# Each expert job of a mixture in two halves, with a branch of its own for each half

## The chip, the cores and the metric

The kernel runs on one core of one Trainium2 chip. The metric is the device time of one execution in microseconds (us). The time of a kernel is the median of its runs.

## The reference

Linear attention is followed by two mixtures of experts; the second takes the output of the first. The change touches the first mixture alone.

```
def _moe_ref(x, w_gate, w1, w2, capacity):        # x 1152 x 512, 8 experts, w1 512 x 1024, w2 1024 x 512
    logits = x @ w_gate
    expert_idx = np.argmax(logits, axis=1)        # one expert for each token
    ...
    disp = np.zeros((E, capacity, D))             # capacity 288 rows for each expert
    ...
    h = np.maximum(np.einsum('ecd,edf->ecf', disp, w1), 0.0)
    y = np.einsum('ecf,efd->ecd', h, w2)
    ...
    out[i] = gate_w[i] * y[expert_idx[i], pos[i]]
```

How many tokens an expert gets is known only when the gate has been computed on the chip.

## The kernel before

Every float32 operand is kept as two parts, a high one (names with H) and a low one (L), and each product is made by `three()` with three matmuls, on lines 198 to 200: high by high, high by low, low by high. All engines run programs of their own, and each engine's program has its own branches.

**The jobs.** The first mixture is a loop over 8 experts (lines 803 to 818), unrolled in the program. Each expert is a job, and each job stands in the program twice, one after the other: as a wide job for up to 288 tokens (`job_wide`) and as a narrow one for up to 128 (`job_narrow`). On each engine a compare-and-branch on the number of tokens (line 810) either goes on into the wide arm, at whose end an unconditional branch jumps over the narrow arm, or jumps over the wide arm to the narrow one. With the inputs of the runs the jobs are, in order, wide, wide, narrow, narrow, wide, narrow, narrow, narrow (the wide ones have matmuls of 288 columns, the narrow ones of 256). Behind the last job a branch of the same kind (line 1133) leads to the second mixture, of which two versions stand in the program.

**A wide job.** The first product has 8 blocks of 128 hidden features, each 4 x 3 matmuls into one PSUM bank; ScalarE evicts a block to `h1H` (line 586), VectorE to `h1L` (line 587). The second product has 4 blocks of 8 x 3 matmuls, which are evicted to `x2H` and `x2L`; behind each of the first three come transposes of the next job's tokens (`win_T`, line 668, 3 matmuls for each of 4 column blocks, from `xw` to `x1H`, `x1L`).

**A narrow job** has the operands of the matmuls swapped, so that tokens come out as rows. The first product has 4 groups of 12 matmuls of 128 x 256; ScalarE evicts each to `hn` (line 724). `turn_h` transposes `hn` back, 4 matmuls of line 715 for groups 0 and 1 (behind the last group), and 4 for groups 2 and 3; they are split into `h1H` and `h1L` (lines 193, 194). Between the two stand `win_T` for column blocks 0 and 1. The second product has 2 groups of 24 matmuls, `win_T` of blocks 2 and 3, the load of the tokens of the job after the next (`win_load`, line 660, one DMA of 576 KB from `xe` to `xw`), and 4 transposes of the result (line 753).

So the wide arm has 96 + 96 + 12 = 204 matmuls, the narrow arm 48 + 4 + 6 + 4 + 48 + 6 + 4 = 120. In the program of TensorE a matmul is two instructions, a weight load and a multiplication.

**Weights.** `wt.split` turns one raw tile of an expert's weights into its two parts (lines 155 and 158; ScalarE makes the high part, VectorE or GpSimd the low one) and then issues the DMA of the next expert's tile into the same raw tile. A job splits the `w1H`, `w1L` that its own second product needs during its first product, and the next job's `w0H`, `w0L` during its second.

**PSUM.** `bank()` hands out the banks of a ring of five in turn (`ring["n"]` counts). Both arms start with the same count, and go on after it with the wide arm's.

Of the kernel before, what the change touches and what calls it, by code (L numbers as in the profile page):

```python
# [20 lines left out]
def kernel(  # L21
# [18 lines left out]
    E, _, F = moe_w1.shape  # L40
    P = 128
# [70 lines left out]
    ring = {"use": pb[0:4], "n": 0}  # L112

    def bank(n):
        ring["n"] += 1
        return ring["use"][ring["n"] % len(ring["use"])][:, 0:n]
# [75 lines left out]
    def split2(hi, lo, src):  # L192
        nc.scalar.activation(out=hi, in_=src, func=AF.Copy)
        nc.vector.tensor_tensor(out=lo, in0=src, in1=hi.bitcast(F32), op=ALU.subtract)

    def three(ps, a, b, i, n):
        (aH, aL), (bH, bL) = a, b
        nc.tensor.matmul(ps, lhsT=aH, rhs=bH, start=i == 0, stop=False)  # L198
        nc.tensor.matmul(ps, lhsT=aH, rhs=bL, start=False, stop=False)  # L199
        nc.tensor.matmul(ps, lhsT=aL, rhs=bH, start=False, stop=i == n - 1)  # L200
# [382 lines left out]
    def evict_split(hi, lo, ps, relu=False):  # L583
        if not relu:
            return split2(hi, lo, ps)
        nc.scalar.activation(out=hi, in_=ps, func=AF.Relu)
        nc.vector.scalar_tensor_tensor(
            out=lo, in0=ps, scalar=0.0, in1=hi.bitcast(F32), op0=ALU.max, op1=ALU.subtract)
# [20 lines left out]
    def wide(t):  # L609
        return t.rearrange("p (a f) -> p a f", f=P)  # L610

    def operands(g):
        return tuple(wide(t) for t in sp0[4 * (g % 2):4 * (g % 2) + 4])

    def prep(g, tmp=None):
        e, p = divmod(g, 4)
        sH, sL, aH, aL = operands(g)
        r = wt.raw[0, p].rearrange("p a (b h f) -> p (a b) h f", h=2, f=P)
        a11, a12, a21, a22 = r[:, 0:2, 0, :], r[:, 2:4, 0, :], r[:, 0:2, 1, :], r[:, 2:4, 1, :]
        parts = [(slice(0, 4), r[:, :, 0, :])] + (  # L620
            [(slice(4, 6), a22)] if g else [(slice(4, 8), r[:, :, 1, :])])
        tt = nc.gpsimd.tensor_tensor
        for o, w in parts:
            nc.scalar.activation(out=aH[:, o, :], in_=w, func=AF.Copy)  # L624
        if g:
            s1, s2, s3, s4 = (wide(tmp)[:, 2 * k:2 * k + 2, :] for k in range(4))
            tt(out=s1, in0=a21, in1=a22, op=ALU.add)
            tt(out=s2, in0=s1, in1=a11, op=ALU.subtract)
        yield
        if g:  # L630
            tt(out=s3, in0=a11, in1=a21, op=ALU.subtract)
            tt(out=s4, in0=a12, in1=s2, op=ALU.subtract)
        yield
        for o, w in parts:
            tt(out=aL[:, o, :], in0=w, in1=aH[:, o, :].bitcast(F32), op=ALU.subtract)  # L635
        if g:
            nc.scalar.activation(out=sH, in_=wide(tmp), func=AF.Copy)
        yield
        if g:
            tt(out=sL, in0=wide(tmp), in1=sH.bitcast(F32), op=ALU.subtract)  # L640
        yield

    with ExitStack() as mctx:
# [9 lines left out]
        def win_load(j):  # L653
            if j >= len(jobs):
                return
            e, w = jobs[j]
            r0 = e * CW + w * W
            step = P if j == 0 else DM
            for o in range(0, DM, step):
                nc.sync.dma_start(  # L660
                    out=xw[:, :, o:o + step], in_=xe[r0:r0 + W, o:o + step].rearrange("(a p) d -> p a d", p=WP))

        def win_T(j, c):
            if j >= len(jobs):
                return
            ps = bank(W)
            for a in range(3):
                nc.tensor.transpose(  # L668
                    ps[:, a * WP:(a + 1) * WP], xw[:, a, c * P:(c + 1) * P], ident[0:WP, 0:WP])
            split2(*x1[c], ps)  # L670

        def job_wide(j, off_r):
            i, w = jobs[j]
            for kk, f in enumerate(FO):
                ps = bank(W)
                for c in range(NC):
                    three(ps, wt.w1(f, c), x1[c], c, NC)
                evict_split(h1H[:, kk, :], h1L[:, kk, :], ps, relu=True)
                if i > 0 and kk < 4 and w == 0:
                    wt.split(i, 1, kk)  # L680
            pg = prep(0)
            for d in range(NC):
                ps = bank(W)
                for kk, f in enumerate(FO):
                    wH, wL = wt.w2(f)
                    three(ps, (wH[:, d * P:(d + 1) * P], wL[:, d * P:(d + 1) * P]),
                          (h1H[:, kk, :], h1L[:, kk, :]), kk, NFC)
                evict_split(x2H[:, d, ds(off_r, W)], x2L[:, d, ds(off_r, W)], ps)
                for c in ((0, 1), (2,), (3,), ())[d]:
                    win_T(j + 1, c)  # L690
                if d == 2:
                    win_load(j + 2)
                if w == NW - 1:
                    if i + 1 < E:
                        wt.split(i + 1, 0, d)
                    else:
                        next(pg)

        def job_narrow(j, off_r):
            i, w = jobs[j]  # L700
            pool = {(1, 3), (0, 1), (0, 3)}

            pg = prep(0)

            def split(i, which, p):
                if i == E:
                    next(pg)
                else:
                    wt.split(i, which, p, nc.gpsimd if (which, p) in pool else None)

            def turn_h(g):
                ps = bank4()
                for f in range(4):
                    o = f % 2 * P
                    nc.tensor.transpose(ps[:, f, :], hn[2 * g + f // 2][:, o:o + P], ident)
                split2(h1H[:, 4 * g:4 * g + 4, 0:P], h1L[:, 4 * g:4 * g + 4, 0:P], ps)

            if i > 0:
                split(i, 1, 0)
            for p in range(4):  # L720
                ps = bank(256)
                for c in range(NC):
                    three(ps, (x1[c][0][:, 0:P], x1[c][1][:, 0:P]), wt.w1p(p, c), c, NC)
                nc.scalar.activation(out=hn[p], in_=ps, func=AF.Relu)
                if i > 0 and p < 3:
                    split(i, 1, p + 1)
                if p == 1:
                    ring["n"] += 1
                if p == 2:
                    turn_h(0)  # L730
            win_T(j + 1, 0)
            win_T(j + 1, 1)
            turn_h(1)
            ring["n"] += 1
            split(i + 1, 0, 0)
            split(i + 1, 0, 1)
            for g in range(2):
                ps = bank(256)
                for kk, f in enumerate(FO):
                    wH, wL = wt.w2(f)  # L740
                    n = slice(g * 256, (g + 1) * 256)
                    three(ps, (h1H[:, kk, 0:P], h1L[:, kk, 0:P]), (wH[:, n], wL[:, n]), kk, NFC)
                nc.scalar.activation(out=yn[g], in_=ps, func=AF.Copy)
                if g == 0:
                    win_T(j + 1, 2)
                    split(i + 1, 0, 2)
            win_T(j + 1, 3)
            win_load(j + 2)
            ring["n"] += 1
            ps = bank4()  # L750
            for c in range(NC):
                o = c % 2 * P
                nc.tensor.transpose(ps[:, c, :], yn[c // 2][:, o:o + P], ident)
            split(i + 1, 0, 3)
            split2(x2H[:, :, ds(off_r, P)], x2L[:, :, ds(off_r, P)], ps)
# [31 lines left out]
        def scalar(src, j, engines=None):  # L787
            return nc.values_load(
                src[0:1, j:j + 1], min_val=0, max_val=N, skip_runtime_bounds_check_because=why,
                **({"engines": engines} if engines else {}))  # L790

        kept_r = scalar(kept_i, 0)
        counts = [scalar(cnt_i, j) for j in range(E)] if NW == 1 else None
# [3 lines left out]
        for t, eng in ((x2H, nc.gpsimd), (x2L, nc.vector)):  # L797
            for c in range(NC):
                for o in range(0, N, 512):
                    n = min(512, N - o)  # L800
# [2 lines left out]
        nc.sync.dma_start(out=tokc, in_=tk.rearrange("(t p) o -> p t o", p=P))  # L803
        for j in range(len(jobs)):
            off_r = scalar(off_i, j, DYN)
            if NW > 1:
                job_wide(j, off_r)
                continue
            n0 = ring["n"]
            with tc.If(counts[j] > P) as cmp:  # L810
                job_wide(j, off_r)
            n1, ring["n"] = ring["n"], n0
            with cmp.Else():
                job_narrow(j, off_r)
            ring["n"] = n1

    skp = ctx.enter_context(tc.tile_pool(name="skp", bufs=1))
    gms = skp.tile([P, 96], F32, name="gms")
# [348 lines left out]
```

## Time and profile before

| | |
|---|---|
| median of 3 runs | 1029.74 us (1029.55 to 1030.85) |
| the profiled execution | 1028.67 us |
| its span, first to last instruction | 1027.0 us |
| TensorE matmul (PE), busy | 966.4 us, 94 % |
| VectorE (DVE), GpSimd (POOL), ScalarE (ACT), busy | 604.6, 412.9, 372.3 us |
| mean granted clock of TensorE | 0.974 |
| DMA, mean over the span | 87 GB/s |

The median is 1.07 us above the profiled execution, and that is 1.67 us longer than its span. Of the span, the first mixture's jobs 2 to 7 take some 208 to 337 us from its start. PE stands for the matmuls, PEld for the weight loads that overlap with them, PEldq for the sequencer that reads TensorE's program; SP issues DMAs. The busy times are sums over stages of the kernel with different limits.

### The profile page before, as it was taken

How to read it: one execution, taken by the hardware profiler on the slowest of the kernel's cores; microseconds unless marked ns; L12 is line 12 of the kernel's file. 1: busy time of each engine (PE TensorE's matmuls, PEld its weight loads, DVE VectorE, ACT ScalarE, POOL GpSimd, SP SyncE). 2: the span in 40 equal slices, each digit the busy share in tenths (PEclk: the TensorE clock that was granted, in tenths of full speed). 3: DMA queues.
4: the chain of work that ended last, by engine and by line, in shares of the span. 5: the costliest groups of instructions: out<-in, count | busy, mean ns of one | idle time of the engine just before them, and what ended most of it. 6: DMA issues, size and time to landing. Idle time of an engine off the chain costs nothing.

```text
span 1027.0 us, 14033 instructions
## 1 busy us (share of the span) xinstructions
PE 966.4 (94%) x5329; PEld 841.8 (82%) x5329; DVE 604.6 (59%) x1074; ACT 372.3 (36%) x621; POOL 412.9 (40%) x398
## 2 busy tenths in 40 slices
PE   8999969978888878999999999999999999999997
PEld 8999968968877656888888888888888888888886
DVE  4667764656554557855565556555655565556555
ACT  4456513566365332233223222322232223222320
POOL 2344243023033535435533553455345434543433
PEclk9999989999998889999999999999999999999999
DMA  7697121579686201111211221122112211110002
GB/s 125 150 276 236 62 89 31 179 212 241 200 230 192 79 21 62 51 41 56 68 42 41 61 63 42 41 62 62 41 41 62 63 41 42 61 41 1 1 1 82
DMA packets 123292, 89.68 MB, mean 87 GB/s; under 512 B 34528, under 2 KB 101344, under 8 KB 123200
## 3 DMA queue, kind: packets, MB, share of 16 engines
q1 hardware_dynamic: 120240, 83.65, 28.9%
q0 software_dynamic: 1728, 4.73, 1.2%
q8 instruction: 55, 0.90, 0.4%
q14 instruction: 37, 0.30, 0.1%
q10 hardware_dynamic: 1232, 0.10, 0.1%
HBM read 79.01 MB, written 9.45 MB: 86 GB/s over the span
## 4 chain that ended last, share of the span: by engine, by line
PE 80%; issue 8%; DVE 7%; ACT 2%; POOL 2%; DMA 1%; ACTq 0%; POOLq 0%; DVEq 0%; SPq 0%
PE pb L995 27%; PE pb L198 15%; PE pb L199 14%; PE pb L200 14%; PE pb L310 3%; PE pb L445 3%; PE pb L428 1%; POOL out_dram L177 1%; DVE hidL L1031 1%; PE pb L254 1%; PE pb L668 1%; DMA wg<-in_moe_w_gate_dram 0%; DVE w1L L158 0%; DVE x2L L801 0%; DVE dq L291 0%
## 5 line engine op out<-in xcount | busy, mean ns | idle before, releaser
L1022 DVE SCALAR_TENSOR_TENSOR oc<-pb,Pm,oc 128x512 f32<-128x512 f32 x224 | 167.1, 749 | 93.8 <-PE pb L200 91.5
L949 POOL TENSOR_TENSOR w1L<-raw,w1H 128x1024 fp32r<-128x1024 f32 x32 | 77.2, 2412 | 345.7 <-ACT w1H L948 345.7
L198 PE MATMUL pb<-w1H,hidH 128*128 128x512 f32 x512 | 199.8, 390 | 0.5 <-DVE hidL L1031 0.5
L199 PE MATMUL pb<-w1L,hidH 128*128 128x512 f32 x512 | 199.7, 390 | 0.0
L200 PE MATMUL pb<-w1H,hidL 128*128 128x512 f32 x512 | 199.6, 390 | 0.0
L1030 ACT ACTIVATE hidH<-snap 128x512 fp32r<-128x512 f32 x93 | 58.8, 632 | 240.7 <-DVE snap L1110 110.1
L995 PE MATMUL pb<-x2H,w0H 128*128 128x512 f32 x310 | 122.6, 396 | 0.0
L995 PE MATMUL pb<-x2L,w0H 128*128 128x512 f32 x310 | 121.7, 392 | 0.0
L995 PE MATMUL pb<-x2H,w0L 128*128 128x512 f32 x310 | 121.5, 392 | 0.0
L198 PEld LDWEIGHTS pb<-w1H,hidH 128*128 128x128 f32 x512 | 96.5, 189 | 20.7 <-DVE hidL L1031 0.6
L199 PEld LDWEIGHTS pb<-w1L,hidH 128*128 128x128 f32 x512 | 96.4, 188 | 20.1
L200 PEld LDWEIGHTS pb<-w1H,hidL 128*128 128x128 f32 x512 | 96.4, 188 | 20.1
L1031 DVE SCALAR_TENSOR_TENSOR hidL<-snap,hidH 128x512 fp32r<-128x512 f32 x93 | 65.7, 706 | 65.0 <-ACT hidH L1030 65.0
L640 POOL TENSOR_TENSOR w0L<-stmp,w0H 128x1024 fp32r<-128x1024 f32 x31 | 74.8, 2414 | 1.6 <-DMA raw<-in_moe_w_dram 1.6
L995 PEld LDWEIGHTS pb<-x2H,w0L 128*128 128x128 f32 x310 | 58.8, 190 | 12.4
L995 PEld LDWEIGHTS pb<-x2H,w0H 128*128 128x128 f32 x310 | 58.7, 189 | 11.9
L995 PEld LDWEIGHTS pb<-x2L,w0H 128*128 128x128 f32 x310 | 58.8, 190 | 11.8
L158 POOL TENSOR_TENSOR w1L<-raw,w1H 128x1024 fp32r<-128x1024 f32 x9 | 21.5, 2384 | 109.5 <-ACT w1H L155 109.2
L635 POOL TENSOR_TENSOR w0L<-raw,w0H 128x512 fp32r<-128x512 f32 x64 | 64.7, 1033 | 0.2 <-ACT w0H L624 0.2
L1030 ACT ACTIVATE hidH<-pb 128x512 fp32r<-128x512 f32 x35 | 20.9, 597 | 96.2 <-PE pb L995 91.3
L1098 ACT COPY snap<-pb 128x512 f32<-128x512 f32 x31 | 18.2, 587 | 83.7 <-PE pb L995 83.7
L995 PE MATMUL pb<-w1H,w0L 128*128 128x512 f32 x124 | 48.3, 389 | 0.0
(246 smaller groups left out, 1999.9 us busy)
## 6 DMA issues: line engine op xcount, KB each, us to landing
raw<-in_moe_w_dram SPq DMA_DIRECT2D x128, 256.0 KB, 3.5
raw<-in_moe_w_dram SPq DMA_DIRECT2D x64, 512.0 KB, 3.8
xe<-zero SPq DMA_DIRECT2D x18, 256.0 KB, 4.2
xw<-xe SPq DMA_DIRECT2D x7, 576.0 KB, 6.9
v<-in_v_dram SPq DMA_DIRECT2D x8, 256.0 KB, 4.9
q<-in_q_dram SPq DMA_DIRECT2D x8, 256.0 KB, 5.2
k<-in_k_dram SPq DMA_DIRECT2D x7, 256.0 KB, 4.9
xw<-xe SPq DMA_DIRECT2D x4, 144.0 KB, 2.5
```

The source lines that it names most:

```text
L198: nc.tensor.matmul(ps, lhsT=aH, rhs=bH, start=i == 0, stop=False)
L199: nc.tensor.matmul(ps, lhsT=aH, rhs=bL, start=False, stop=False)
L200: nc.tensor.matmul(ps, lhsT=aL, rhs=bH, start=False, stop=i == n - 1)
L310: nc.tensor.matmul(kvps[b][g // 4][:, g % 4, 0:MW], lhsT=kp[:, h, half, :], rhs=vv[:, h * VW:h * VW + MW], start=first and g % 4 == 0, sto ...
L445: nc.tensor.matmul(ps[:, h, 0:MW], lhsT=qt[:, g, :], rhs=kv[b][:, g * KW:g * KW + MW], start=half == 0, stop=half == 1,)
L635: tt(out=aL[:, o, :], in0=w, in1=aH[:, o, :].bitcast(F32), op=ALU.subtract)
L640: tt(out=sL, in0=wide(tmp), in1=sH.bitcast(F32), op=ALU.subtract)
L949: nc.gpsimd.tensor_tensor(out=lo, in0=r, in1=hi.bitcast(F32), op=ALU.subtract)
L995: nc.tensor.matmul(o, lhsT=a[x][:, c, :], rhs=b[c][y], start=first and c == 0 and m == 0, stop=c == 1 and m == 2, skip_group_check=True)
L1022: nc.vector.scalar_tensor_tensor(out=o, in0=ps, scalar=gate, in1=o, op0=ALU.mult, op1=ALU.add)
L1030: nc.scalar.activation(out=hi, in_=src, func=AF.Relu)
L1031: nc.vector.scalar_tensor_tensor(out=lo, in0=src, scalar=0.0, in1=hi.bitcast(F32), op0=ALU.max, op1=ALU.subtract)
```

## The change

Both functions become generators with one `yield`: the wide job's stands between its two products, the narrow job's between the transposes of groups 0 and 1 and the first `win_T`. The loop takes each job in two steps, and each step has a branch of its own on the same count, with the first half of the wide job and the first half of the narrow job as its arms, then the second halves.

```
@@ job_wide
                 if i > 0 and kk < 4 and w == 0:
                     wt.split(i, 1, kk)
+            yield
             pg = prep(0)
             for d in range(NC):
@@ job_narrow
                 if p == 2:
                     turn_h(0)
+            yield
             win_T(j + 1, 0)
             win_T(j + 1, 1)
             turn_h(1)
@@ the loop over the jobs
             off_r = scalar(off_i, j, DYN)
+            wide_job = job_wide(j, off_r)
             if NW > 1:
-                job_wide(j, off_r)
+                for _ in wide_job:
+                    pass
                 continue
-            n0 = ring["n"]
-            with tc.If(counts[j] > P) as cmp:
-                job_wide(j, off_r)
-            n1, ring["n"] = ring["n"], n0
-            with cmp.Else():
-                job_narrow(j, off_r)
-            ring["n"] = n1
+            narrow_job = job_narrow(j, off_r)
+            for _ in range(2):
+                n0 = ring["n"]
+                with tc.If(counts[j] > P) as cmp:
+                    next(wide_job, None)
+                n1, ring["n"] = ring["n"], n0
+                with cmp.Else():
+                    next(narrow_job, None)
+                ring["n"] = n1
```

The program then holds, for each job, in this order: wide first half (96 matmuls), narrow first half (52), wide second half (108), narrow second half (68). The count of the ring is set to the wide arm's at the border too, so that the second half of a narrow job gets other banks than before.

Two places in TensorE's program; waits stand in brackets, and "x3" counts like instructions. The first is the border of a wide job, here job 4. Before:

```order
L200 MATMUL pb_128<-x1H_1888,w0L_149 128x288
L198 MATMUL pb_129<-h1H,w1H_150 128x288 [waits DVE_49]
L199 MATMUL pb_129<-h1L,w1H_150 128x288
L200 MATMUL pb_129<-h1H,w1L_151 128x288
L198 MATMUL pb_129<-h1H,w1H_150 128x288 [waits Activation_49]
L199 MATMUL pb_129<-h1L,w1H_150 128x288
L200 MATMUL pb_129<-h1H,w1L_151 128x288
```

After (the line of the branch has become 816):

```order
L816 UNCONDITIONAL_BRANCH
L816 COMPARE_AND_BRANCH
L198 MATMUL pb_129<-h1H,w1H_150 128x288 [waits DVE_49,Activation_49]
L199 MATMUL pb_129<-h1L,w1H_150 128x288 [waits DVE_49]
L200 MATMUL pb_129<-h1H,w1L_151 128x288
L198 MATMUL pb_129<-h1H,w1H_150 128x288
L199 MATMUL pb_129<-h1L,w1H_150 128x288
```

The second matmul of the second product now has a wait on VectorE, and the later ones no more waits on ScalarE; between the products stands the narrow job's first half, with the two branches around it.

The second place is the border of a narrow job, here job 2; `turn_h` is line 716 after the change. Before:

```order
L668 MATMUL pb_130<-ident,xw 128x96 [waits DMAHW7_49,DMAHW5_49]
L668 MATMUL pb_130<-ident,xw 128x96 x2
L668 MATMUL pb_126<-ident,xw 128x96 x3
L715 MATMUL pb_127<-ident,hn_1894 128x128 [waits Activation_49]
L715 MATMUL pb_127<-ident,hn_1894 128x128
```

After:

```order
L668 MATMUL pb_127<-ident,xw 128x96 [waits DMAHW5_49,DVE_49,DMAHW7_49,Activation_49]
L668 MATMUL pb_127<-ident,xw 128x96 x2
L668 MATMUL pb_128<-ident,xw 128x96 [waits DVE_49]
L668 MATMUL pb_128<-ident,xw 128x96 x2
L716 MATMUL pb_129<-ident,hn_1894 128x128 [waits Activation_49]
L716 MATMUL pb_129<-ident,hn_1894 128x128
```

`turn_h` for groups 0 and 1 writes `pb_128` before and after; the second `win_T` now takes the same bank and has a wait on VectorE.

## Rows read from the trace of the kernel before

**Rows 1.** Page, the chain that ended last: shares of the span by engine.

```profile
PE 80%; issue 8%; DVE 7%; ACT 2%; POOL 2%; DMA 1%; ACTq 0%; POOLq 0%; DVEq 0%; SPq 0%
```

**Rows 2.** Windows, jobs 3, 4, 7: us, busy PE PEld DVE ACT POOL, PEclk, DMA share, GB/s.

```profile
233.94:249.53 15.59, 15.59 (x121) 15.29 (x122) 8.10 (x10) 10.40 (x19) 4.90 (x2) 0.91 0.87 229
249.53:276.10 26.57, 26.57 (x205) 26.34 (x203) 15.63 (x24) 13.61 (x24) 2.40 (x1) 1.00 0.70 207
...
321.26:337.23 15.97, 15.40 (x108) 14.67 (x108) 3.84 (x4) 7.28 (x13) 4.94 (x3) 0.87 0.65 198
```

**Rows 3.** Timeline of PE: start, duration, instruction, in brackets idle before and its releaser.

```profile
213.23 0.55 PE L198 MATMUL pb<-w0H,x1H 128*128 128x256 f32 x1 [4.78 <-DVE w1L L158]
...
233.94 0.55 PE L198 MATMUL pb<-w0H,x1H 128*128 128x256 f32 x1 [5.06 <-DVE w1L L158]
...
296.78 0.35 PE L198 MATMUL pb<-w0H,x1H 128*128 128x256 f32 x1 [0.33 <-DVE x1L L194]
...
301.86 0.28 PE L199 MATMUL pb<-w0L,x1H 128*128 128x256 f32 x1 [0.80 <-issue]
...
307.38 0.44 PE L668 MATMUL pb<-ident,xw 96*128 96x96 f32 x3 [3.25 <-DMA xw<-xe]
...
321.26 0.55 PE L198 MATMUL pb<-w0H,x1H 128*128 128x256 f32 x1 [4.33 <-DVE w1L L158]
```

**Rows 4.** Timeline of DVE, job 6: start, duration, instruction, idle before.

```profile
298.74 4.32 DVE L158 TENSOR_TENSOR w1L<-raw,w1H 128x1024 fp32r<-128x1024 f32 x3 [0.32 <-ACT w1H L155]
```

**Rows 5.** Line 810's branches on PE's sequencer: ns min/median/max, first to last start.

```profile
L810 PEldq COMPARE_BRANCH  x2: 286/3546/6807, 205.9 to 206.3; - x2
...
L810 PEldq COMPARE_BRANCH  x1: 601/601/601, 296.0 to 296.0; - x1
...
L810 PEldq COMPARE_BRANCH  x1: 4549/4549/4549, 316.5 to 316.5; - x1
```

**Rows 6.** The DMA queue of instruction fetches: packets, MB, share; a long stretch, then 293 to 296.

```profile
437.50:1014.00 576.50, 576.50 (x2546) 477.34 (x2545) 336.11 (x481) 169.30 (x258) 260.97 (x220) 1.00 0.15 43
...
q8 instruction: 20, 0.33, 0.2%
...
q8 instruction: 1, 0.02, 2.0%
```

**Rows 7.** The branch to the second mixture, line 1133, on PE's sequencer.

```profile
L1133 PEldq COMPARE_BRANCH  x1: 3484/3484/3484, 336.8 to 336.8; - x1
```

**Rows 8.** Windows of the halves of narrow jobs, and of an idle stretch of the DMA engines.

```profile
296.78:304.13 7.35, 6.55 (x52) 6.25 (x52) 5.01 (x4) 6.20 (x10) 2.79 (x2) 1.00 1.06 249
241.47:249.53 8.06, 8.06 (x71) 7.76 (x70) 5.65 (x8) 6.12 (x13) 4.69 (x2) 1.00 0.83 253
307.38:316.93 9.55, 9.54 (x68) 9.06 (x68) 4.58 (x7) 5.62 (x11) 2.48 (x1) 0.82 0.76 246
...
284.00:287.00 3.00, 3.00 (x25) 3.00 (x25) 1.52 (x2) 2.08 (x4) 0.00 (x0) 0.90 0.11 33
```

**Rows 9.** Timeline at the borders of the products: wide job 1 (PE, DVE), narrow job 3.

```profile
194.44 0.30 PE L198 MATMUL pb<-h1H,w1H 128*128 128x288 f32 x1
...
195.08 0.46 DVE L587 SCALAR_TENSOR_TENSOR h1L<-pb,h1H 128x288 fp32r<-128x288 f32 x1 [1.13 <-ACT h1H L586]
...
241.47 0.66 PE L668 MATMUL pb<-ident,xw 96*128 96x96 f32 x6
...
241.70 0.69 DVE L194 TENSOR_TENSOR h1L<-pb,h1H 128x512 fp32r<-128x512 f32 x1 [0.70 <-ACT h1H L193]
```

**Rows 10.** The load of the tokens: issues on SP, and the four landing times of 208 to 334.

```profile
229.21 1.47 SPq L660 DMA_DIRECT2D xw<-xe  x1
...
297.13 0.67 SPq L660 DMA_DIRECT2D xw<-xe  x1
...
DMA to landing us min/median/max: 8.2/9.2/10.1
```

## The prediction

> **What bounds the kernel now.** I read the chain of waits first: four fifths of it is PE, 8 % is "issue", time in which nothing that the profile shows was waited for [rows 1]. So the end moves with what PE does or misses; other engines matter where PE waits for them. Then I cut the first mixture into its jobs [rows 2]. Job 4, wide, has PE busy in every microsecond, at a granted clock of 1.00. Narrow job 3 has 15.6 us from its first matmul on and a clock of 0.91; job 7 has 15.97 at 0.87.
>
> Next I asked in PE's timeline what stood ahead of each narrow job's first matmul [rows 3]: nothing ran on PE for 4.78, 5.06 and 4.33 us ahead of jobs 2, 3 and 7 (job 5 is like them, job 4 ended at 276.10 and its first matmul came within the same bounds), but only for 0.33 us ahead of job 6. Wide jobs have no such gap. The releaser column names a low part of the weights (`w1L`, DVE, line 158) each time. I don't believe it. In job 6 the first matmul ran at 296.78, while `w1L` was only made from 298.74 on [rows 4]: the first product doesn't wait for it. The column falls back on the last semaphore, and what ended last is seen on PE's own sequencer. Its compare-and-branch over the wide arm took 6.81 us into job 2, 4.55 into job 7, and lay between these for jobs 3 and 5; into job 6, which has the only short gap, it took 0.60 [rows 5]. The unconditional branch over the narrow arm, at the end of wide job 1, took 0.29 us (the least of the pair at 206).
>
> So a long jump costs 4.5 to 6.8 us, a short one 0.3. Why is job 6 the exception? In the long stretch of the second mixture the queue of instruction fetches brought 20 packets of 16 KB for 2546 matmuls and 2545 weight loads [rows 6]: 5091 / 20 = about 255 instructions a packet. A steady stream fetches blocks of 256 just ahead; just before job 6's jump, within 293 to 296, one packet came [rows 6]. I read it so: on entering a block PE fetches the next one and no more, and a jump that lands in a block neither present nor on its way is refilled at full price. The jump over the wide arm skips 204 matmuls, some 411 instructions with waits and branch, more than a block and a half. Counting instructions, job 6's jump left from early in a block, and landed in the one just fetched.
>
> **What the change removes.** The jumps become shorter. Over a wide first half there are 96 matmuls, 194 instructions; over the wide second half 108, 219; over the narrow halves 52 and 68 matmuls, 106 and 139. All are under 256, so each lands in the block that it leaves or in the next one, whose fetch began when the block was entered. The price of a jump is then between 0.3 (fetch done) and a miss less what ran since. By my count of instructions, with the borders of the blocks laid where the packets of the trace come, three of the ten taken jumps leave shortly behind a border: the one at the middle of job 2 (15 instructions after it), the one into job 5 (13) and the one into job 6 (44, which is some 22 matmuls of 0.13 us, job 4's 26.57 / 205 [rows 2], 2.8 us of cover). Job 6's jump as it is gives the scale: 26 instructions behind a border, a branch of 0.60, a gap of 0.33. The new jumps at 15 and 13 have some 6 matmuls, 0.8 us, less cover, so I estimate gaps of 1.0, 1.0 and 0.3 us, each between 0.3 and the 4.5 of a miss. The jump into the second mixture (3.48 us, [rows 7]) is as long as ever; I put 0.5 us on it, for PE arrives there without other work.
>
> The branches here took between 0.29 and 6.81 us [rows 5], as far apart as a hit and a miss. The Trainium skill, "Advanced Engine Details and Errata", section "Control Flow Timing", has 51 ns for a branch and 108 ns for a compare-and-branch, and by that no jump costs microseconds: the change would remove nothing, and only what it adds would be left (rival 3).
>
> What a narrow job costs without a gap: first half 7.35 less the 0.80 inside it = 6.55, at a clock of 1.00 [rows 3, 8]; second half 8.06 [rows 8]; together 14.6. A second half behind a wait of 3 us took 9.55, at 0.82 [rows 8].
>
> **What it adds.**
> - Wide borders. The second matmul of the second product now waits for the last `h1L`. In job 1 the second product began at 194.44, while that eviction ran from 195.08 for 0.46 us, to 195.54 [rows 9]. PE would start its second matmul about 1.15 us later than now, with only the first under the wait; bounds 0.8 and 1.6. Three wide jobs: +3.4 us. Queued behind it is the whole second product, so it is on the path.
> - Narrow borders. The second `win_T` now takes the bank out of which VectorE is making `h1L`: 241.70 + 0.69 = 242.39, while all six transposes stood at 241.47 with 0.66 us [rows 9]. Three transposes of 0.11 us run first: about +0.6 a job (0 to 0.7), where nothing later is waited for.
> - Two more branches a job, 0.07 to 0.31 us each; most of it behind queued matmuls. I put 0.3 on each taken jump and nothing on one not taken.
>
> **What is late next.** Gaps that vanish on PE run into the load of the tokens. Inside job 6, the one narrow job that entered without a gap, the first `win_T` waited 3.25 us for `xw` [rows 3]: issued at 297.13, it needed 10.1 us; the four loads of this stretch took 8.2 to 10.1 [rows 10]. It is issued at the end of the job before and can't start earlier, since `xw` has one buffer. The DMA engines are busy to a share of 0.83 to 1.06 in such halves [rows 8]. But they have an idle stretch ahead of them, in job 5 284 to 287 (share 0.11) [rows 8], and one like it in job 2, which stand there because PE came late: an earlier PE frees raw tiles earlier, and these 3 us can be filled. So `xw` follows PE, but not by all of it.
>
> **The sum.** Jobs 2 and 3, now 208.44 to 249.53 [rows 2, 3]. Job 2: 0.3 + 14.6 + 0.6 + 1.0, end at 224.9. Job 3's first half: 0.3 + 6.55, at 231.8. Its `xw` is issued 0.3 behind job 2's end, as now (229.21 against 228.88 [rows 10, 3]), and lands 9.2 us later, at 234.4; a second half behind a wait, 9.55, ends at 244.0. Gain 5.5, less 0.3 at job 4's start: 5.2.
>
> Jobs 5 to 7, now 276.10 to 337.23. Job 5: 1.0 + 14.6 + 0.6, end at 292.3. Job 6's first half: 0.3 + 6.55, at 299.15. `xw` landed at 297.13 + 10.1 = 307.2; issued 0.7 behind job 5's end, as now, and with the same 10.1 it would be 303.1, by the 2.7 us that the idle stretch can take (3.00 x 0.89) 304.5; I take the later. Plus 9.55: 314.05. Job 7: 0.3 + 14.0 (its 15.97 us hold 15.40 of work at a clock of 0.87 [rows 2]; at 1.00 that is 0.13 x 15.4 = 2.0 less), end at 328.35. Gain 8.9, less 0.5 at the second mixture: 8.4.
>
> 5.2 + 8.4 - 3.4 = 10.2. The profiled execution of 1028.67 becomes 1018.5; the median of the runs lies 1.07 above it: **1019.6 us**, ratio 0.990. The forecast holds from about 1014 to 1024.5: the three partial fetches between 0.3 and a miss, the wide borders between 2.4 and 4.8, `xw` 1 us to either side.
>
> **The rivals.**
> 1. *The whole gap comes back.* The loads move as early as PE does, and the wait for `xw` is gone in both trains. Jobs 2, 3: 16.5 + 15.5 = 32.0 instead of 41.1, gain 8.8 with job 4's start; jobs 5 to 7: 16.2 + 15.5 + 14.3 = 46.0 instead of 61.1, gain 14.6 with the second mixture; less 3.4: 20.0, 1009.7 us. For it: idle DMA stretches. Against it: job 6, which had no gap, waited all the same. 0.15.
> 2. *The DMA paces the narrow jobs.* `xw` lands no earlier than now: 238.4 in job 3 (229.21 + 9.2) and 307.2 in job 6. Gains 1.3 and 5.5, less 3.4: 3.4, 1026.3 us. For it: shares near 1 in the halves in question. Against: the share of 0.11 ahead of them. 0.15.
> 3. *The other side: the gaps are data waits, as the releaser column says, and jumps are free.* Then no gap goes, and what stays is 3.4 at the wide borders and 0.6 in four narrow jobs: +5.8, 1035.5 us. It decides if the gaps stay at 4 to 5 us while the branches ahead of them are short. Against it stand job 6's `w1L` and the durations of the branches [rows 5]. I give it 0.05.
> 4. *Each taken jump refills, wherever it lands.* Five more of them at about 4.7, plus 3.4: 1056.6 us. Against it: the 0.29 and 0.60 among the branches. 0.02.
> 5. *Nothing measurable:* the partial fetches cost near a full miss each (3 us more each) on top of rival 2's late loads. 0.05.
>
> The forecast has 0.58. 0.2 % (2 us) is about what a measurement of this kernel can tell from no change. Faster by more: the forecast and rivals 1 and 2, 0.88; within it rival 5, 0.05; slower rivals 3 and 4, 0.07. For 8 in 10 I take the forecast, rival 2 and the half of rival 1 in which some wait for `xw` is left: 0.58 + 0.15 + 0.08 = 0.81, 1010 to 1027.
>
> **What would show it.** Right: no compare-and-branch on PE in jobs 2 to 7 above some 3 us, the gaps of 4 to 5 us ahead of jobs 2, 3 and 7 down to about 0.3, the long wait of jobs 3 and 6 at the first `win_T`, released by `xw`, 2.5 to 4.5 us; a gap of about 1 us behind the first matmul of each wide second product, released by `h1L`; job 7's clock nearer to 1. Wrong: branches of over 4 us at the new borders (blocks lie elsewhere than counted, or a jump inside the next block still misses), `win_T` waiting less than 1 us (rival 1) or more than 6 (rival 2), or the gaps unchanged with short branches (rival 3).

## The result, and the profile after

The changed kernel took 1017.12 us (median of 4 runs, 1015.67 to 1021.61) against 1029.89 us before in the same runs: ratio 0.9895, 95 % interval 0.9868 to 0.9922. The forecast was 1019.6 us, ratio 0.990, range 1010 to 1027. The profiled execution took 1015.94 us with a span of 1013.8; the sum of the prediction had 1018.5 for it.

In the changed kernel's profile the chain of waits has less "issue" and more DMA than in [rows 1]:

```profile
PE 81%; DVE 6%; issue 5%; DMA 3%; ACT 2%; POOL 2%; ACTq 0%; SPq 0%; POOLq 0%; DVEq 0%
```

The branches on PE's sequencer (line 816 now; ns min/median/max) answer to [rows 5]. Those into job 2 (210.8), job 3 (229.1), job 5 (272.6), job 6 (290.8), the middle of job 6 (296.0) and into job 7 (308.1) take 0.2 to 0.6 us, but for 1.32 into job 5; in the two rows with "x2" the shorter one is the jump at the end of the wide job before. The jumps in the middle of jobs 2, 3, 5 and 7 took 0.2 to 0.4 us. Only the branch to the second mixture, line 1139, is long, as in [rows 7]:

```profile
L816 PEldq COMPARE_BRANCH  x2: 169/252/334, 210.6 to 210.8; - x2
L816 PEldq COMPARE_BRANCH  x1: 416/416/416, 229.1 to 229.1; - x1
L816 PEldq COMPARE_BRANCH  x2: 187/753/1319, 272.3 to 272.6; - x2
L816 PEldq COMPARE_BRANCH  x1: 219/219/219, 290.8 to 290.8; - x1
L816 PEldq COMPARE_BRANCH  x1: 645/645/645, 296.0 to 296.0; - x1
L816 PEldq COMPARE_BRANCH  x1: 318/318/318, 308.1 to 308.1; - x1
...
L1139 PEldq COMPARE_BRANCH  x1: 4318/4318/4318, 322.8 to 322.8; - x1
```

PE's timeline shows what is idle now, against the gaps of 4 to 5 us in [rows 3]. The first matmuls of jobs 2, 3, 5, 6 and 7 (212.94, 229.69, 274.70, 291.22, 308.57) have 0.15 us or less ahead of them. What is left stands inside the jobs:

```profile
186.76 0.40 PE L198 MATMUL pb<-x1H,w0H 128*128 128x288 f32 x1 [1.17 <-DVE w0L L158]
...
199.13 0.40 PE L199 MATMUL pb<-h1L,w1H 128*128 128x288 f32 x1 [0.86 <-DVE h1L L587]
...
215.82 0.39 PE L198 MATMUL pb<-w0H,x1H 128*128 128x256 f32 x1 [1.28 <-DVE w0L L158]
...
221.66 0.39 PE L668 MATMUL pb<-ident,xw 96*128 96x96 f32 x2 [0.58 <-DVE h1L L194]
...
238.38 0.44 PE L668 MATMUL pb<-ident,xw 96*128 96x96 f32 x3 [1.82 <-DMA xw<-xe]
...
300.42 0.36 PE L668 MATMUL pb<-ident,xw 96*128 96x96 f32 x2 [2.11 <-DMA xw<-xe]
...
327.30 0.77 PE L198 MATMUL pb<-x2H,w0H 128*128 128x512 f32 x1 [4.05 <-issue]
```

The fifth and sixth are the waits for `xw` in jobs 3 and 6, the second is the wide border of job 1 (job 4 has the same 0.86), the fourth the narrow border of job 2 (job 5 the same). The first and the third, 1.2 to 1.3 us at the second group of matmuls of jobs 1, 2 and 5, were not forecast.

The windows of jobs 3, 6 and 7, the second halves of 3 and 6, and the stretch that was idle on the DMA engines in [rows 8] (columns as in [rows 2]):

```profile
229.69:246.29 16.60, 14.55 (x120) 13.91 (x121) 10.51 (x12) 12.29 (x22) 7.25 (x3) 1.00 1.00 287
...
291.22:308.57 17.35, 14.78 (x121) 13.92 (x121) 11.05 (x13) 12.75 (x22) 7.24 (x3) 1.00 1.00 283
308.57:323.25 14.68, 13.79 (x108) 12.82 (x108) 6.64 (x7) 9.31 (x16) 7.33 (x4) 1.00 0.79 247
...
238.38:246.29 7.91, 7.91 (x68) 7.64 (x69) 4.79 (x6) 5.49 (x11) 2.67 (x2) 1.00 0.94 318
300.42:308.57 8.15, 8.10 (x68) 7.63 (x69) 5.00 (x7) 5.75 (x11) 2.48 (x1) 1.00 0.97 331
...
283.00:286.00 3.00, 2.60 (x23) 2.59 (x23) 1.97 (x5) 2.36 (x6) 1.57 (x1) 1.00 0.95 336
```

The granted clock is 1.00 in all of them, where jobs 3 and 7 had 0.91 and 0.87, and the DMA engines are full where they had stood idle.

### The profile page after: what moved, and what is told of

Its sections match the earlier page's. It is cut to its first block, busy times and chain, and to the rows that moved or that the text cites. A ratio compares the mean times of both kernels' runs of the same rounds, so it can differ in the third digit from the quotient of the medians.

```text
span 1013.8 us, 14074 instructions
## 1 busy us (share of the span) xinstructions
PE 962.8 (95%) x5329; PEld 836.5 (83%) x5329; DVE 603.8 (60%) x1074; ACT 372.4 (37%) x621; POOL 413.1 (41%) x398
## 4 chain that ended last, share of the span: by engine, by line
PE 81%; DVE 6%; issue 5%; DMA 3%; ACT 2%; POOL 2%; ACTq 0%; SPq 0%; POOLq 0%; DVEq 0%
PE pb L1001 27%; PE pb L198 15%; PE pb L199 15%; PE pb L200 14%; PE pb L310 3%; PE pb L445 3%; DMA xw<-xe 2%; PE pb L428 1%; PE pb L668 1%; POOL out_dram L177 1%; DVE hidL L1037 1%; PE pb L254 1%; DMA wg<-in_moe_w_gate_dram 1%; DVE x2L L194 0%; DVE dq L291 0%
## 5 line engine op out<-in xcount | busy, mean ns | idle before, releaser
L1001 PEld LDWEIGHTS pb<-x2H,w0H 128*128 128x128 f32 x310 | 58.7, 189 | 11.9
L1001 PE MATMUL pb<-w1H,w0H 128*128 128x512 f32 x124 | 48.5, 391 | 0.0
```

The lines of the kernel that those rows point to most:

```text
L1001: nc.tensor.matmul(o, lhsT=a[x][:, c, :], rhs=b[c][y], start=first and c == 0 and m == 0, stop=c == 1 and m == 2, skip_group_check=True)
```

## The experiments

Three sets of runs, each with its own runs of the kernel before, on chips that differ: before took 1028.4 us in the first set, 1024.4 in the second, 1023.3 in the third. So kernels of different sets are compared by their ratio to before.

| set | run | median us | ratio to before | 95 % interval |
|---|---|---|---|---|
| 1 | again (the changed kernel) | 1017.2 | 0.9882 | 0.9847 to 0.9916 |
| 1 | border | 1014.45 | 0.9857 | 0.9828 to 0.9887 |
| 1 | ring | 1015.7 | 0.9885 | 0.9852 to 0.9919 |
| 1 | ringborder | 1013.4 | 0.9859 | 0.9828 to 0.9890 |
| 2 | swap | 1024.87 | 1.0004 | 0.9989 to 1.0019 |
| 2 | dead | 1035.09 (one run) | | |
| 2 | xw2 | 1007.48 | 0.9831 | 0.9809 to 0.9854 |
| 2 | best | 999.54 | 0.9766 | 0.9739 to 0.9793 |
| 3 | again2 (the changed kernel) | 1012.84 | 0.9897 | 0.9877 to 0.9917 |
| 3 | bxw2 | 1024.31 | 1.0012 | 0.9993 to 1.0031 |
| 3 | long | 1067.03 | 1.0419 | 1.0390 to 1.0447 |
| 3 | best2 | 995.18 | 0.9726 | 0.9703 to 0.9748 |

**Were the gaps jumps?** The run swap is the kernel before with the narrow arm first.

```
-            with tc.If(counts[j] > P) as cmp:
-                job_wide(j, off_r)
+            with tc.If(counts[j] < P + 1) as cmp:
+                job_narrow(j, off_r)
...
             with cmp.Else():
-                job_narrow(j, off_r)
+                job_wide(j, off_r)
```

> The kernel before, one branch a job, but with the narrow arm first in the program: a wide job now jumps over the narrow arm (244 instructions) at its start, a narrow one over the wide arm (411) at its end. Jump theory: the 4 to 5 us in front of jobs 2 and 5, which follow a wide job, vanish; those in front of jobs 3 and 7 stay, now inside an unconditional branch of PE of 4 us or more; job 4, which follows a narrow one and had no gap, gets one, and so does the way from job 7 to the second mixture; one of them may be spared as job 6's was. The sum is about that of before, 1024 to 1034 us. Data theory (the gaps wait for weights): the gaps stay in front of jobs 2, 3, 5 and 7, none comes in front of job 4.

Measured: ratio 1.0004. In the timeline of PE the gaps are where the long jumps are; ahead of jobs 2 and 5 (204.25 and 279.09) nothing is idle, and wide job 4 and the second mixture have one. These are the first matmuls of jobs 3, 4, 6, 7 and of the second mixture, with a later one in job 4, the third row, and behind them the branch ahead of job 4:

```profile
223.28 0.55 PE L198 MATMUL pb<-w0H,x1H 128*128 128x256 f32 x1 [4.66 <-DVE w1L L158]
...
244.62 0.58 PE L198 MATMUL pb<-x1H,w0H 128*128 128x288 f32 x1 [4.95 <-issue]
...
251.22 0.61 PE L200 MATMUL pb<-x1H,w0L 128*128 128x288 f32 x1 [5.07 <-issue]
...
297.88 0.55 PE L198 MATMUL pb<-w0H,x1H 128*128 128x256 f32 x1 [4.43 <-DVE w1L L158]
314.90 0.36 PE L198 MATMUL pb<-w0H,x1H 128*128 128x256 f32 x1 [0.41 <-DVE x1L L194]
...
337.26 0.77 PE L198 MATMUL pb<-x2H,w0H 128*128 128x512 f32 x1 [8.12 <-issue]
...
L810 PEldq COMPARE_BRANCH  x1: 4902/4902/4902, 239.2 to 239.2; - x1
```

The releaser column still names `w1L` in two of them, on jobs that follow other jobs than before. The data theory has fallen. The gap of 5.07 us inside job 4 stands at no jump, but 1.5 us of work behind the landing of one, and the queue of instruction fetches brought one packet within it; more on such stalls below.

The run dead prices the length of a jump: the kernel before, with branches over code that never runs, in its wide jobs.

```
+        SKIPS = {(1, 0): 40, (1, 2): 150, (4, 0): 110, (4, 2): 300}
...
+                if (j, d) in SKIPS:
+                    with tc.If(counts[j] > N - 1):
+                        keep_warm(SKIPS[j, d])
```

> The kernel before, and in its wide jobs 1 and 4 four branches over code that never runs, 40 and 150 matmuls long in job 1 (82 and 302 instructions), 110 and 300 in job 4 (222 and 602), behind the first and the third group of the second product. Nothing else is added there. Jump theory: PE's taken branches over 82 and 222 instructions take under 1.5 us, those over 302 and 602 take 3.5 to 7 us, most of it seen as a gap on PE. Rival (a jump costs nothing by itself): all four take 0.3 us or less.

Its branches over 82, 302, 222 and 602 instructions, in this order:

```profile
L692 PEldq COMPARE_BRANCH  x1: 225/225/225, 190.5 to 190.5; - x1
...
L692 PEldq COMPARE_BRANCH  x1: 1803/1803/1803, 197.8 to 197.8; - x1
...
L692 PEldq COMPARE_BRANCH  x1: 411/411/411, 262.8 to 262.8; - x1
...
L692 PEldq COMPARE_BRANCH  x1: 4407/4407/4407, 270.1 to 270.1; - x1
```

On the sequencer 82 and 222 took 0.2 and 0.4 us, 602 took 4.4. 302 came out at 1.8, below the 3.5 that I had expected; as I read it, it can still land in the next block, with its fetch on the way. PE itself had matmuls queued and idled less than expected: 2.04 us behind the branch over 602, nothing that shows behind the one over 302. One profile, with each length once, but the four are in order.

```profile
274.66 0.35 PE L668 MATMUL pb<-ident,xw 96*128 96x96 f32 x2 [2.04 <-PEq L692]
```

The run long keeps the split with all its waits and makes the jumps long again: 220 instructions that never run at the end of both wide halves.

```
+            unused(j)
             yield
...
+        def unused(j):
+            with tc.If(counts[j] > N - 1):
+                keep_warm(110)
```

> The changed kernel, with code that never runs (110 matmuls, 220 instructions) at the end of both halves of the wide job. The borders, the waits and the banks are those of the changed kernel, but the narrow jobs' jumps are 416 and 441 instructions long. Jump theory (the gain is the shortness of the jumps and nothing else of the split): most of the ten taken jumps of the narrow jobs miss, five of them in the middle of a job, 3 to 5 us each as a gap, of which xw's wait hides two: 1035 to 1055 us, slower than before. Rival (the split helps by something else, as an earlier start of transfers): 1018 to 1024 us, for the three wide jobs' own jumps.

Measured: ratio 1.0419, 54 us above the changed kernel in the same set. The narrow jobs' ten taken branches took 3.7 to 5.5 us each; those of jobs 2 and 3, into the job and at its middle:

```profile
L822 PEldq COMPARE_BRANCH  x1: 5531/5531/5531, 218.4 to 218.4; - x1
...
L822 PEldq COMPARE_BRANCH  x1: 4781/4781/4781, 229.8 to 229.8; - x1
...
L822 PEldq COMPARE_BRANCH  x1: 5357/5357/5357, 243.9 to 243.9; - x1
...
L822 PEldq COMPARE_BRANCH  x1: 4077/4077/4077, 256.1 to 256.1; - x1
```

PE idled for 4.7 to 8.4 us at the starts of the narrow jobs and for 2.1 to 3.0 in their middles; those of job 3:

```profile
249.45 0.55 PE L198 MATMUL pb<-w0H,x1H 128*128 128x256 f32 x1 [5.09 <-DVE w1L L158]
...
260.43 0.27 PE L668 MATMUL pb<-ident,xw 96*128 96x96 f32 x1 [2.10 <-issue]
```

It is slower than expected: 54 us above the changed kernel, where the upper end of the range was 38 above it. The wide jobs share in that, which I had taken as nearly free: at the end of a half PE jumps over the added code in 0.3 to 0.4 us, and the jump over the narrow half that follows it takes 2.4 to 3.0 us in five halves of six, though it skips only 106 or 139 instructions. So a short jump right behind another isn't cheap. The gain is the shortness of the jumps; the split without it loses.

**What do the new waits come from?** In the run border the wide job's `yield` stands behind the first 24 matmuls of the second product (the count of the ring is taken back by one in the narrow job).

```
-            yield
             pg = prep(0)
             for d in range(NC):
...
+                if d == 0:
+                    yield
```

> As the changed kernel, but the wide job's border stands behind the first 24 matmuls of the second product, where the last h1L has long been made; the jumps stay under 256 instructions (242 and 171). Theory (the wide borders cost because the second half's first matmuls wait for the last work of the half before): the waits of 0.86 us in jobs 1 and 4 and some 2.1 of the 3.8 us in job 0 go, the second products start at once, 4 us less than the changed kernel: about 1013 us. Rival (the loss at the borders is the branch or the fetch of instructions itself): the gap moves along with the border and nothing is won, 1017 us.

In the run ring the narrow job takes its banks in another order.

```
-                if p == 1:
-                    ring["n"] += 1
                 if p == 2:
+                    ring["n"] += 4
                     turn_h(0)
+                    ring["n"] -= 3
...
             turn_h(1)
-            ring["n"] += 1
...
             win_load(j + 2)
-            ring["n"] += 1
```

> As the changed kernel, but the narrow job takes the PSUM banks in another order: no bank is skipped in its second half, so that its last bank is not the one that the next job's second group of matmuls uses, and turn_h for groups 0 and 1 takes a bank that the second half uses late. Theory (the waits of 1.17 and 1.28 us at the second group of jobs 1, 2 and 5 and of 0.58 at the second win_T come from the shifted ring, and are waits for the end of the other half and arm, not for data of their own): these five go, some 4.9 us, of which xw gives back 1 to 2 in jobs 3 and 6: 1013 to 1014 us. Rival (the second group needs the w0L of which the releaser column speaks): the waits stay where they are, 1017 us.

The run ringborder has both edits.

> Both edits together. Theory: the two gains stand at different places of PE's path and add up, less what xw gives back in jobs 3 and 6: 1008 to 1011 us. Rival (one common limit, for instance the loads of weights, sets the pace of the mixture): no better than the better one of the two alone.

> The changed kernel once more, as the scale for the other three. Its four runs so far lay between 1015.7 and 1021.6 us, a wider spread than before's 1.3 us. If the spread comes from how the loads of the narrow jobs happen to meet, the median stays near 1017 with a spread of several us, and a profile with a longer time has longer waits for xw or longer branches, not longer wide jobs.

The times of this set spread by 7 to 9 us within a kernel, so the intervals of all four overlap, and the medians decide nothing between them. By the medians border, ring and ringborder came out above what was expected of them (about 1013, 1013 to 1014, and 1008 to 1011 us), border and ring by less than the spread. The spread has more than one source: in the profile of again job 3 waited 3.80 us for `xw` instead of 1.82, and the whole mixture began 1.9 us later. What the edits do is read from the profiles. In border the second products of jobs 1 and 4 take 13.84 us with PE busy throughout; with the wait they take 14.97 (here in again2):

```profile
199.26:213.10 13.84, 13.84 (x110) 13.84 (x109) 6.97 (x11) 5.74 (x11) 0.00 (x0) 1.00 0.33 96
260.55:274.39 13.84, 13.84 (x111) 13.84 (x109) 6.97 (x11) 5.69 (x11) 0.00 (x0) 1.00 0.30 89
```

```profile
192.51:207.48 14.97, 14.11 (x111) 13.88 (x109) 6.96 (x11) 5.74 (x11) 0.00 (x0) 1.00 0.30 88
```

So a wide border costs 1.13 us, and the border of the halves need not cost it. In job 0 the 2.1 us expected did not come: there border's PE waited 4.84 us for ScalarE, behind the first matmuls of the second product.

```profile
171.37 0.61 PE L198 MATMUL pb<-h1H,w1H 128*128 128x288 f32 x1 [4.84 <-ACT h1H L586]
```

In ring the second group of job 2 starts at 213.46, in step with the matmuls ahead of it, while VectorE made the last `w0L` only from 213.62 for 1.23 us (PE, then DVE):

```profile
213.46 0.28 PE L198 MATMUL pb<-w0H,x1H 128*128 128x256 f32 x1
```

```profile
213.62 1.23 DVE L158 TENSOR_TENSOR w0L<-raw,w0H 128x1024 fp32r<-128x1024 f32 x1 [0.49 <-ACT w0H L155]
```

The group doesn't need that `w0L`; the wait was one for a bank that the narrow arm of the half before uses last. It was met by the end of VectorE's work in that half: in the changed kernel PE went on at 215.82, when this instruction, the half's last on VectorE, had just ended.

```profile
214.54 1.23 DVE L158 TENSOR_TENSOR w0L<-raw,w0H 128x1024 fp32r<-128x1024 f32 x1 [0.49 <-ACT w0H L155]
```

All five waits that the expectation names are gone in ring's profile. But ring pays elsewhere: `turn_h` now waited 0.5 to 0.8 us in each of the five narrow jobs for an eviction from the bank that I had given it, and job 2 has a stall in the middle of its second half:

```profile
223.77 0.45 PE L716 MATMUL pb<-ident,hn 128*128 128x128 f32 x1 [3.87 <-issue]
```

The branch ahead of it took 0.34 us, and the queue of instruction fetches brought one packet within the gap. A border of a block just behind a jump's landing costs nearly as much as a missed jump: that is how I read it; no run moves that border alone. The 5.07 us in job 4 of swap, 3.87 in job 7 of dead and 3.30 in job 2 of ringborder look the same, each with one such packet in the gap.

**What is late next?** The run xw2 is the changed kernel with two buffers for the tokens.

```
+        xw2 = [x1p.tile([WP, 3, DM], F32, name=f"xw{k}") for k in range(2)]
...
+            win_load(j + 2)
             win_T(j + 1, 0)
...
             win_T(j + 1, 3)
-            win_load(j + 2)
```

(in the wide job it stands at `d == 0` instead of 2.)

> The changed kernel with two buffers for the tokens, whose load is issued at the start of the second half instead of at its end, half a job earlier. Theory (what is late next is xw): the waits of 1.8 to 3.8 us in job 3 and 2.1 us in job 6 at the first win_T go, 4 to 5 us: about 1012.5 us. Rival (the DMA paces the narrow jobs, and the tokens only take the place of weights): the wait comes back as one for weights elsewhere in the narrow jobs, 1016 us or more.

Measured: ratio 0.9831 against 0.9897 of the changed kernel (again2), 0.0066 or some 6.8 us, where 4 to 5 were expected; the two ratios are of different sets, and their intervals leave some 3 us of it open. The first `win_T` of job 3 waits for nothing (the row is the second, at the narrow border), the one of job 6 for 0.26 us:

```profile
232.54 0.47 PE L668 MATMUL pb<-ident,xw 96*128 96x96 f32 x3 [0.58 <-DVE h1L L194]
...
292.54 0.44 PE L668 MATMUL pb<-ident,xw 96*128 96x96 f32 x3 [0.26 <-DMA raw<-in_moe_w_dram]
```

The same edit on the kernel before is the run bxw2.

> The kernel before, one branch a job, with the two buffers for the tokens alone. Theory (the refills of PE's instructions hide the load of the tokens, and only job 6, which is spared the refill, waits for it): 3.25 us at most are won, ratio 0.997 to 1.000, and the gaps of 4 to 5 us stay. Rival (the second buffer is worth its 5 us by itself, by moving the loads): ratio 0.994 to 0.995, as between the changed kernel and the run named xw2.

Measured: 1.0012, no gain. The gaps stay; job 6 has lost its wait for `xw`, but now has a gap of 2.45 us at its start, since its jump was no longer spared (a branch of 2.72 us instead of 0.60), and the gap into job 3 has grown. These are the first matmuls of jobs 3 and 6:

```profile
230.64 0.55 PE L198 MATMUL pb<-w0H,x1H 128*128 128x256 f32 x1 [7.95 <-issue]
...
295.60 0.55 PE L198 MATMUL pb<-w0H,x1H 128*128 128x256 f32 x1 [2.45 <-ACT w1H L155]
```

The gaps ahead of the five narrow jobs add up to 22.8 us, against 19.0 in the profile of before (one profile each, on different chips): the refills took back what `xw` gave. Why they grew is not shown. With the refills the second buffer was worth nothing, without them some 6.8 us.

**A version that beats both.** The run best has the later border, the banks of ring with `turn_h` moved out of the way (`+= 3`, `-= 2`), and the two buffers.

> The later border of the wide job, the narrow job's banks (turn_h of groups 0 and 1 now in the bank of the group before the last one, where it waited 0.5 to 0.8 us in the run named ring) and the two buffers for the tokens together. Theory: 2 us for the wide borders, 5 for the banks, 4 for xw: 1006 to 1009 us. Rival: stalls of PE's instruction fetch take some of it back where a border of a block falls just behind a jump's landing: 1010 to 1013 us.

The run best2 has in addition the two versions of the second mixture in the other order.

```
-    with tc.If(kept_r > N - P) as cmp:
+    with tc.If(kept_r < N - P + 1) as cmp:
...
+            moe2_fast(fp)
     with cmp.Else():
```

> The run named best, with the two versions of the second mixture in the other order in the program, so that the one that runs comes first. Theory: PE's branch of 3.4 to 4.4 us between the mixtures becomes one of less than 0.3, 3.5 to 4 us less than best. Rival: the jump over the other version now stands at the program's end, and the last work behind it waits as long: no gain.

> The changed kernel on the chip of the next three, as their scale. On the last chip before took 1024.4 us instead of 1028 to 1030, and kernels without the changed borders had no stall of ScalarE at the end of job 0's first product. If that stall belongs to the chip and not to the kernel, the changed kernel's ratio to before stays at 0.988 to 0.990 here too.

Measured: best 0.9766, best2 0.9726 (995.18 us), against 0.9897 for the changed kernel in best2's set, which is within the 0.988 to 0.990 expected of again2. Best is 0.0131 or some 13 us below the changed kernel, across two sets, where 8 to 11 were expected. The step from best to best2 is 0.0040, 4 us, across two sets whose intervals just overlap. The branch between the mixtures is short in best2 (4.25 us in best), and the jump at the program's end gave nothing back that the time shows:

```profile
L1139 PEldq COMPARE_BRANCH  x1: 73/73/73, 308.4 to 308.4; - x1
...
309.58 0.47 PE L198 MATMUL pb<-x2H,w0H 128*128 128x512 f32 x1 [0.78 <-ACT x2H L193]
```

Short jumps are not free in these versions either. The one in the middle of job 6 took 2.25 us in best and 3.25 in best2, where PE idled for 1.17 us behind it:

```profile
L816 PEldq COMPARE_BRANCH  x1: 3245/3245/3245, 282.5 to 282.5; - x1
...
285.96 0.35 PE L668 MATMUL pb<-ident,xw 96*128 96x96 f32 x2 [1.17 <-DMA raw<-in_moe_w_dram]
```

## Why the prediction was right, step by step

- **Gaps are missed jumps, and short jumps hit.** Right: swap, dead and long. The rivals that all gaps are data waits, and that every jump refills, have fallen. A branch on PE took 0.07 us here where it wasn't taken, and 0.2 to 8.2 where it was. The figures of the Trainium skill, "Advanced Engine Details and Errata", section "Control Flow Timing", 51 ns for a branch and 108 for a compare-and-branch, are not the whole price of a taken branch here. Rivals 1 and 2, all of the gap or little of it, missed on `xw`: it kept 3.9 us, neither nothing nor all, and less than the 2.5 to 4.5 a job that the prediction gave as a sign of being right. Rival 5, nothing measurable, fell with the 12.8 us.
- **Where the blocks lie.** Of the three jumps that were counted as leaving just behind a border, only the one into job 5 shows it, with a branch of 1.32 us; the one in the middle of job 2 took 0.22, the one into job 6 0.22. The positions were counted rightly only in part.
- **Jobs 2 and 5.** Forecast 16.5 and 16.2 us; they took 16.6 (213.10 to 229.69) and 16.4. The total is right and its parts are not: the partial fetches at the two starts and the middle cost almost nothing that PE shows (0.3 + 1.0 forecast), and the unforecast wait of 1.28 us at the second group stands in their place; that the totals agree is luck. The 0.6 at the narrow border was 0.58.
- **`xw`.** Its place was right, its size not. Job 3's first half ended on time (6.9 us after its start), and `xw` cost 1.82 us where the sum had 2.6. In job 6 it cost 2.11 where the sum had 5.35: the estimate that `xw` could move ahead only by the 2.7 us of the idle stretch was too tight. It was issued at 292.12 and PE went on at 300.42, 8.3 us later instead of 10.1, with the DMA engines moving 283 GB/s over the job, against 249 and 246 in the halves of before's job 6 [rows 8]. Over both jobs this is the term most off, by 4.0 us.
- **The second half behind a wait.** Off as well: 9.55 us each, taken from the half that followed a wait of 3.25 us at a clock of 0.82. The two halves took 7.91 and 8.15, at 1.00: 3.0 us of the gain that I had not counted.
- **Wide jobs.** 3.4 forecast, 6.3 in the profile. The borders of jobs 1 and 4 cost 1.13 each (1.15 forecast). Job 0's second half was 2.04 us longer, and jobs 1 and 4 lost 1.41 and 0.68 in their first halves, most of it the same wait as in jobs 2 and 5 and a start behind `x2L`. Job 0's share isn't the border alone: there ScalarE stood idle for 3.90 us ahead of the last `h1H` (1.18 in bxw2), and already in the profile of before that half took 18.13 us. On the third set's chip it took 13.85 without a border (bxw2) and 14.98 with one (again2), 1.13 again. PE waited 2.1 to 5.4 us at this place in the profiles of before, of the changed kernel and of set 1, and 0.9 at most in those of sets 2 and 3; what held ScalarE up stays open.
- **Net.** Forecast 5.2 + 8.4 - 3.4 = 10.2; in the profiles 7.7 + 11.9 - 6.3 = 13.3 (the end of job 1 to the start of job 4, 208.44 to 249.34, became 213.10 to 246.29; the end of job 4 to the second mixture, 276.10 to 340.44, became 274.86 to 327.30). The trains of narrow jobs gave 6.0 more, the wide jobs took 2.9 more. So the mechanism was right and most of its sizes were not; that 1019.6 came within 2.5 us of 1017.12 is partly luck, since two errors of opposite sign met. The branch to the second mixture took 4.32 us instead of 3.48 [rows 7], a loss of 0.84 where 0.5 stood.

## What to carry to other kernels

A branch on a hot engine has a price that depends on how far it jumps and, as I read it, on how long ago the last block was entered. On PE's sequencer here most jumps over up to some 240 instructions took 0.2 to 0.6 us and some took 1.2 to 3.3; those over 411 and more took 3.5 to 8.2, but for four that were spared in part (0.3 to 2.7). So split long arms, or put the likely one where it is fallen into. Cut where the next half's first instructions need nothing of the half's last work, and don't let the last PSUM bank of one arm be an early bank of the next half, since such a wait was met here only by the end of the half's work on VectorE. And look for the transfer that the removed stall was hiding: two buffers were worth nothing before the change and some 6.8 us after it.

## What the runs showed of the hardware that was not expected

- TensorE's clock: gaps of 4 to 5 us went with windows at 0.91 and 0.87 [rows 2], waits of up to 2.1 us inside jobs 3 and 6 left them at 1.00. Part of a stall's price is what follows it.
- The releaser column names a semaphore that came last, and did so for gaps that instruction fetch made. The durations of the branches on PE's sequencer told them apart.
